# List work behind the attention of a step, output weights loaded by SyncE, last activation finished behind the next pair's copy: one change to a tuned attention and two-layer kernel

## The chip, the cores and the metric

The kernel runs on one core of a Trainium2 chip. Its time is device microseconds of one execution. The kernel before took 919.52 us (median of three runs, 918.92 to 920.69). Five engines run their own instruction streams and meet at semaphores: TensorE (PE: matmuls into PSUM banks), VectorE (DVE), ScalarE (ACT), GpSimd (POOL) and SyncE (SP, which starts transfers). ACT and POOL can start transfers too; they then stand in that engine's own queue of instructions (ACTq in the profile).

## What is computed

```
ret  = (scale * q @ k.T  *  decay mask) @ v            # 4 batches, 8 heads, 576 tokens, 64 per head
x    = ret as 2304 tokens x 512
h    = x @ w_in;  g = h * sigmoid(1.702 h);  y = g @ w_out            # 512 -> 2048 -> 512
xn   = y / rms(y) * rms_g
gate = xn @ w_gate;  val = xn @ w_val
out  = (gate * sigmoid(gate) * val) @ w_out2                          # 512 -> 1536 -> 512
```

All tensors are float32.

## The kernel before

A float32 operand is held as a high and a low part; each product is three matmuls, high by high, high by low and low by high (`three`, L290 to L292). The parts are made by a rounding copy on ACT and a subtraction on DVE. The attention is computed in chunks with a running state, in 18 units of 128 tokens, and its pieces are laid between the matmuls of the first layer (`attend`: transposes, scores, `a_both` for scores of one unit with outputs of another, `a_out`). L420 (DVE) masks scores, L490 (ACT) and L494 (DVE) move an attention output out of PSUM; until L494 is through, the next hidden product finds no free bank.

The first layer runs over four blocks of tokens, n = 0 to 3. Blocks 0 to 2 have 16 steps f of one 128-wide slice of the hidden layer: attention piece, hidden product (`m1_up`), activation (L646, L626 on ACT, L628 on DVE), and the output product (`down`) of a step two back. Steps with `a_both` run one output product before the hidden product as well. Block 3 (768 tokens) runs in eight pairs of steps (`s_up`): seven half products with sums of the weights and of x in place of eight. L817 copies the first half product on ACT, L802 adds on DVE, `gelu` is L809 and L811 on ACT with L812 on DVE. The gated layer (`m2_up`) uses the same scheme in three blocks of twelve steps; its additions are L1085, its products L1088.

Beside this a list of work (`work`, filled by `in_prep` and `prep`) makes the weight sums ahead of time: load gate and val weights (L179), turn their bytes into words on ACT (`conv_words`, L199 and L200), join them on DVE (L253), add and subtract (L729, L743), split into parts (`split_off`: L716 on ACT, L717 on DVE) and store them (L721) to `sum_d` and `up_d`. `make(slot)` takes as much of the list at the end of a step as a table `room` gives that step. `split_off` goes round the buffers in `FILL[1]` and `FILL[2]` by a running count modulo their number. Output weights of the first layer that are no longer on the chip are loaded again by `w_rot` (L284, 512 KB each) on ACT's queue, into one of three slots. After a block come the norm's scaling (L941) and sums of normalised values for the next half products (L996 for block 0 of the gated layer, L1007 and L1014 for others), handed out by `spread` a few units at a time; at a block's last step (the edge) all that is left is run at once. `first_load` and `x_load` bring x back.

Order on each engine is the order in which this program emits the instructions; there is no scheduler.

Of the kernel before, what the change touches and what calls it, by code (L numbers as in the profile page):

```python
# [10 lines left out]
F32 = mybir.dt.float32  # L11
# [33 lines left out]
def kernel(  # L45
# [225 lines left out]
    def w_rot(n, f):  # L271


        at = A_ROT + (n * NF1 + f) % 3 * 1024
        both, wh, wl = fast[:, at:at + 1024], fast[:, at:at + 512], fast[:, at + 512:at + 1024]
        if ("out", f) in W:
            w = W["out", f][1]
            nc.scalar.copy(out=wh, in_=w)
            nc.vector.tensor_tensor(out=wl, in0=w, in1=wh.bitcast(F32), op=ALU.subtract)
            if n == 1 or f >= NKEEP:  # L280
                w_free("out", f)
                to_store.append(lambda: nc.sync.dma_start(out=out_d[f], in_=both.bitcast(F32)))
        else:
            nc.scalar.dma_start(out=both.bitcast(F32), in_=out_d[f])  # L284
        R["out", f] = (wh, wl)
# [491 lines left out]
    def s_up(p, downs, hook):  # L777
# [29 lines left out]
        def gelu(a, h, t):  # L807
            o = g_tile(TH)
            nc.scalar.activation(out=o, in_=a, func=AF.Gelu_apprx_sigmoid)  # L809
            gh, gl = (x[:, TH * t:TH * t + TH] for x in h)  # L810
            nc.scalar.copy(out=gh, in_=o)  # L811
            return lambda: nc.vector.tensor_tensor(out=gl, in0=o, in1=gh.bitcast(F32), op=ALU.subtract)  # L812

        c1, u2, u3 = side
        a = bank()
        product(a, 0, True)
        nc.scalar.copy(out=c1, in_=a)  # L817
        b = bank()
        product(b, 1, True)
        plus(u2, b, c1)  # L820
        product(a, 2, False)
        gelu(a, h0, 0)()
        hook(0)
# [5 lines left out]
        plus(u3, c, u3)  # L829
        gelu(u3, h1, 1)()  # L830
        hook(1)
        run(downs[1], KD)
        product(b, 5, False)
        plus(c1, b, c1)
        low = gelu(c1, h1, 0)
        product(c, 6, False)
        plus(u2, c, u2)
        low()
        gelu(u2, h0, 1)()

# [341 lines left out]
    with tc.manual_schedule():  # L1182
# [245 lines left out]
        for n, f in ((n, f) for n in (1, 2) for f in range(NF1)):  # L1428
            fn = gap.get((n, f), (None,))[0]
            length = 5.45 + {a_trans: 0.9, a_both: 2.2, a_out: 1.2}.get(fn, 0)  # L1430
            taken = 0.7 + {a_trans: 0.7, a_both: 3.5, a_out: 0.9}.get(fn, 0) + 0.7 * (n == 1 and 0 < f <= NKEEP)
            taken += 1.2 * (4 < f < 14) + (0, 3.8, 3.8, 1.9)[max(0, f - 12) * (n == 2)]
            room[n, f] = max(0, 0.85 * length - taken) * (0 if n == 1 and f < 2 else 0.7 if n == 2 and f < 9 else 1)
        for p in range(NF1 // 2):
            for i in range(2):
                room["last", 2 * p + i] = max(0, (4.8, 2.0)[i] - {0: 1, 1: 1.4, 11: 1.9, 12: 3.8, 13: 1.9, 14: 3.3, 15: 2.3}.get(2 * p + i, 0))

        def make(*slot):

            total = sum(w[0] for w in work)  # L1440
            budget = total * room[slot] / (sum(room.values()) or 1)
            del room[slot]
            slot_no[0] += 1
            while work and budget > work[0][0] / 2 and (len(work[0]) == 2 or work[0][2] in ready):
                cost, op = work.popleft()[:2]
                op()
                budget -= cost
            for f in [f for f in due if due[f] <= slot_no[0]]:
                del due[f]
                conv_words("gate", f)  # L1450
                conv_words("val", f)
                ready.add(f)

        out2_next = [0]
        for n in range(N1 - 1):
            for f in range(NF1):
# [27 lines left out]
                if n > 0 and f == 3:  # L1484
# [3 lines left out]
                    norm += [sq[a:b] for a, b in zip(cuts, cuts[1:])]  # L1488
                if n == 2:
                    if f == 11:  # L1490
                        assert not load_at and wfree == list(range(11)), wfree
# [8 lines left out]
                        sum_load(0)  # L1500
                    if f in (7, 12):
                        for i in range(2):
                            nc.sync.dma_start(
                                out=(fast[:, 4864 + 1536 * i:][:, :2 * TH] if f == 7 else late[:, (768, 5376)[i]:][:, :2 * TH])
                                .bitcast(F32).rearrange("p (k c) -> p k c", k=2),
                                in_=x_d[:, 2 * i:2 * i + 2, TH * (f // 12):][:, :, :TH],
                            )
# [4 lines left out]
                if joined:  # L1512
                    run(down(pending.pop(0)), KD)
                if (n, f) == (0, 0):


                    m1_up(n, f, lambda: conv_join([to_conv.pop(0)]), lambda: conv_words(*to_conv[0]))
                else:
                    m1_up(n, f, lambda: run(rows, 1))
# [4 lines left out]
                else:  # L1524
                    run(spread, 2)
                if n == 2 and f == 13:
                    held_ids = [sfree.popleft() for _ in range(2)]
# [4 lines left out]
                    }, temps, x1, True)  # L1532
                if n == 2 and f > 12:
                    run(sums, 4 if f < 15 else len(sums))
                pending.append((1, n, f))
                if len(pending) > LAG:
                    run(down(pending.pop(0)), KD)
                if n > 0:
                    make(n, f)
            if n == 0:  # L1540
                w_rot(n, NF1 - 1)
        assert not norm
        FILL[2].append(slots(11, 2))
        for s in range(1, NSUM):
            sum_load(s)
        side.extend(norm_tile(nm) for nm in ("c1", "u2", "u3"))
        for p in range(NF1 // 2):
            last = p == NF1 // 2 - 1

            def hook(i):  # L1550
                if i == 0 and p == 0:
                    x_split(temps[1], x1[XT4])
# [4 lines left out]
                if p > 4 and sums:  # L1557
                    run(sums, (0, 2, 4, 2, 2, 1)[2 * p + i - 10])
                if last and i == 0:
                    ring_load(1)  # L1560
                    ring_load(2)
                if last:
                    out2_make(i)
                make("last", 2 * p + i)
                if p > 4 and out2_next[0] < 2:
                    w_load("out2", out2_next[0])
# [3 lines left out]
            w_rot(N1 - 1, 2 * p)  # L1570
            if p == 5:
                held_ids = [sfree.popleft() for _ in range(2)]
                temps = [k_halves(stage(i)[:, :2 * TH]) for i in held_ids]
                raw = {
                    (0, 0): k_halves(fast[:, 16384:][:, :2 * TH]), (0, 1): x_parts(XT3)[1], (1, 0): x_parts(X10)[1],
                    (1, 1): x_parts(X11)[1],
                }
                raw = {k: t.bitcast(F32) for k, t in raw.items()}
                x_load(0, raw)
                sums = x_sums(raw, temps, [x_parts(i) for i in range(7)], False)  # L1580
            if p == 6:
# [13 lines left out]
        for n in range(NBLK):  # L1595
            for f in range(NF2):
# [28 lines left out]
                def hook(i, c=None):  # L1625
# [92 lines left out]
```

## Time and profile before

| | |
|---|---|
| median of three runs | 919.52 us |
| profiled execution | 921.01 us, span 919.3 us |
| mean granted TensorE clock | 0.984 of full speed |
| busy: PE, DVE, ACT, POOL | 884.9, 574.9, 393.1, 38.3 us |
| moved by DMA | 206.61 MB, mean 225 GB/s |

Block 0 to 2 of the first layer take the time to about 349 us, the pairs run to about 490, the gated layer from there on. In a row of the timeline the bracket holds how long the engine stood idle before the instruction, and what it was waiting for; `x` counts the instructions in a row. A row of the waits has the sum, the number and the longest. Matmul durations in the trace overlap, so spacing from start to start tells the pace.

### The profile page before, as it was taken

The numbers are of one execution on the slowest core, as the hardware profiler recorded it, in microseconds if no ns is written. First come the engines' busy times: TensorE is split into PE (matmuls) and PEld (weight loads), VectorE is DVE, ScalarE is ACT, GpSimd is POOL, SyncE is SP. The second block draws the span as 40 slices with busy tenths as digits, with TensorE's granted clock in tenths as the row PEclk, the third lists the DMA queues.
The fourth block names the chain that finished last, engine by engine and source line by source line (L and its number), as shares of the span: only waits on it lengthen the run. The fifth ranks groups of instructions, "written<-read, shape, count | busy, mean of one in ns | idle before, by whom it ended". The sixth has DMA issues, their size and how long they took to land.

```text
span 919.3 us, 16132 instructions
## 1 busy us (share of the span) xinstructions
PE 884.9 (96%) x6122; PEld 782.4 (85%) x6122; DVE 574.9 (63%) x1041; ACT 393.1 (43%) x748; POOL 38.3 (4%) x41
## 2 busy tenths in 40 slices
PE   8999999997988997999998999999999999999998
PEld 7778888885877886899887999989999999999997
DVE  4787746677754677675674567677565666444444
ACT  3777653433443555555454434335323225222222
POOL 2202111021000000000000000000000000000000
PEclk9999999998998998999999999999999999999999
DMA  9997946757898798999947866655855555655553
GB/s 215 247 298 227 253 132 224 247 168 239 259 343 282 218 323 287 339 353 307 349 144 264 270 204 195 206 161 183 275 160 161 161 160 171 219 161 160 161 161 103
DMA packets 166877, 206.61 MB, mean 225 GB/s; under 512 B 73420, under 2 KB 100304, under 8 KB 166800
## 3 DMA queue, kind: packets, MB, share of 16 engines
q1 hardware_dynamic: 160308, 183.68, 64.0%
q10 hardware_dynamic: 6364, 21.64, 6.9%
q8 instruction: 49, 0.80, 0.4%
q0 software_dynamic: 128, 0.27, 0.1%
q14 instruction: 28, 0.23, 0.1%
HBM read 154.15 MB, written 51.38 MB: 224 GB/s over the span
## 4 chain that ended last, share of the span: by engine, by line
PE 73%; DVE 10%; ACT 9%; DMA 5%; issue 2%; ACTq 0%; SPq 0%; POOL 0%; DVEq 0%; POOLq 0%
PE h L290 14%; PE h L292 13%; PE h L291 13%; PE acc L290 7%; PE acc L291 7%; PE acc L292 7%; DMA up_d<-tops 3%; PE v L292 2%; PE v L291 2%; PE v L290 2%; PE at L371 1%; DVE tops L729 1%; ACT sslots L200 1%; ACT g L809 1%; DMA sslots<-in_moe_w_val_dram 1%
## 5 line engine op out<-in xcount | busy, mean ns | idle before, releaser
L290 PE MATMUL h<-fast 128*128 128x384 f32 (+1 forms) x744 | 267.5, 360 | 25.5 <-DVE x L494 11.4
L291 PE MATMUL h<-fast 128*128 128x384 f32 (+1 forms) x744 | 263.1, 354 | 0.7 <-DVE fast L1007 0.7
L292 PE MATMUL h<-fast 128*128 128x384 f32 (+1 forms) x744 | 263.1, 354 | 0.0
L1085 DVE TENSOR_TENSOR tops<-h,tops 128x384 f32<-128x384 f32 x180 | 99.8, 556 | 146.3 <-PE h L292 144.2
L290 PEld LDWEIGHTS h<-fast 128*128 128x128 f32 x744 | 141.6, 190 | 42.8 <-DVE x L494 12.3
L291 PE MATMUL acc<-fast 128*128 128x512 f32 x400 | 157.8, 395 | 0.0
L291 PEld LDWEIGHTS h<-fast 128*128 128x128 f32 x744 | 141.7, 190 | 10.1 <-DVE fast L1007 0.9
L290 PE MATMUL acc<-fast 128*128 128x512 f32 x376 | 149.1, 397 | 0.0
L292 PEld LDWEIGHTS h<-fast 128*128 128x128 f32 x744 | 141.5, 190 | 8.2 <-DVE fast L228 0.2
L292 PE MATMUL acc<-fast 128*128 128x512 f32 x376 | 148.3, 394 | 0.0
L1118 ACT CAST fast<-g 128x384 fp32r<-128x384 f32 x36 | 18.5, 514 | 211.4 <-DVE g L1088 211.4
L291 PEld LDWEIGHTS acc<-fast 128*128 128x128 f32 x400 | 75.8, 189 | 11.9
L292 PEld LDWEIGHTS acc<-fast 128*128 128x128 f32 x376 | 71.2, 189 | 15.4
L290 PEld LDWEIGHTS acc<-fast 128*128 128x128 f32 x376 | 71.2, 189 | 12.6
L628 DVE TENSOR_TENSOR fast<-g,fast 128x512 fp32r<-128x512 f32 x48 | 34.4, 716 | 69.8 <-ACT fast L626 69.8
L716 ACT CAST tops<-tops 128x512 fp32r<-128x512 f32 (+1 forms) x58 | 34.0, 597 | 65.6 <-DVE tops L729 42.4
L646 ACT ACTIVATE g<-h 128x512 f32<-128x512 f32 x48 | 28.4, 592 | 73.1 <-PE h L292 69.0
L291 PE MATMUL v<-fast 128*128 128x512 f32 (+1 forms) x136 | 46.3, 340 | 0.0
L717 DVE TENSOR_TENSOR tops<-tops 128x512 fp32r<-128x512 f32 (+1 forms) x58 | 39.6, 696 | 8.9 <-ACT tops L716 7.3
L292 PE MATMUL v<-fast 128*128 128x512 f32 (+1 forms) x112 | 39.5, 352 | 0.0
L290 PE MATMUL v<-fast 128*128 128x512 f32 (+1 forms) x112 | 39.4, 351 | 0.0
L199 ACT ACTIVATE sslots<-sslots 128x512 f32<-128x512 f32 x56 | 37.6, 671 | 3.8 <-DMA sslots<-in_moe_w_gate_dram 3.1
(189 smaller groups left out, 1136.8 us busy)
## 6 DMA issues: line engine op xcount, KB each, us to landing
fast<-up_d SPq DMA_DIRECT2D x252, 256.0 KB, 3.0
fast<-out_d ACTq DMA_DIRECT2D x41, 512.0 KB, 4.0
up_d<-tops SPq DMA_DIRECT2D x78, 256.0 KB, 5.0
sslots<-in_moe_w_out_dram SPq DMA_DIRECT2D x18, 512.0 KB, 5.6
out_d<-fast SPq DMA_DIRECT2D x16, 512.0 KB, 5.6
sum_d<-tops SPq DMA_DIRECT2D x32, 256.0 KB, 3.4
sslots<-in_moe_w_in_dram SPq DMA_DIRECT2D x15, 512.0 KB, 6.1
fast<-sum_d SPq DMA_DIRECT2D x26, 256.0 KB, 4.6
```

The lines of the kernel that those rows point to most:

```text
L199: nc.scalar.activation(out=hi, in_=hi, func=AF.Prelu, scale=2.0 ** -112, alpha=-(2.0 ** 32))
L200: nc.scalar.activation(out=lo, in_=byte, func=AF.Copy, scale=1 / 32, bias=-31 / 64)
L290: nc.tensor.matmul(ps, lh, rh, start=first, stop=False, skip_group_check=more)
L291: nc.tensor.matmul(ps, lh, rl, start=False, stop=False, skip_group_check=more)
L292: nc.tensor.matmul(ps, ll, rh, start=False, stop=last, skip_group_check=more)
L371: nc.tensor.transpose((more if i == 0 and p > 1 else pt[i])[:, p * 128:(p + 1) * 128], t[:, 2 * p:2 * p + 2, :].rearrange("p h d -> p (h d)"),
L628: nc.vector.tensor_tensor(out=gl, in0=g, in1=gh.bitcast(F32), op=ALU.subtract)
L646: nc.scalar.activation(out=g, in_=ps, func=AF.Gelu_apprx_sigmoid)
L716: nc.scalar.copy(out=wh.bitcast(F32R), in_=w)
L717: nc.vector.tensor_tensor(out=wl.bitcast(F32R), in0=w, in1=wh, op=ALU.subtract)
L1085: nc.vector.tensor_tensor(out=o, in0=a, in1=b, op=ALU.add)
L1118: nc.scalar.copy(out=gh0, in_=g0)
```

## The change

The diff below is cut. `w_rot` issues its load on SyncE. In `s_up` the two last steps of the last activation (copy and subtraction) go to `left` and are run by `last_half` in the next pair (that function is there already for the gated layer). `make` comes right behind the output product in steps with `a_both`, and not at their end; conversions that are due are not run in such a step. The table `room` is new, and so is the number of sums of x per step. `FILL[2]` gets its fourth buffer at step 1 of block 2 and not at its end. In the first block of the gated layer five units of `spread` run per step instead of six.

```diff
@@ w_rot
-            nc.scalar.dma_start(out=both.bitcast(F32), in_=out_d[f])
+            nc.sync.dma_start(out=both.bitcast(F32), in_=out_d[f])
@@ s_up
-            nc.scalar.copy(out=gh, in_=o)
-            return lambda: nc.vector.tensor_tensor(out=gl, in0=o, in1=gh.bitcast(F32), op=ALU.subtract)
+            return (
+                lambda: nc.scalar.copy(out=gh, in_=o),
+                lambda: nc.vector.tensor_tensor(out=gl, in0=o, in1=gh.bitcast(F32), op=ALU.subtract),
+            )
...
         nc.scalar.copy(out=c1, in_=a)
+        last_half(0)
         b = bank()
         product(b, 1, True)
         plus(u2, b, c1)
+        last_half(1)
...
-        gelu(u2, h0, 1)()
+        left.extend(gelu(u2, h0, 1))
@@ room
-            taken = 0.7 + {a_trans: 0.7, a_both: 3.5, a_out: 0.9}.get(fn, 0) + 0.7 * (n == 1 and 0 < f <= NKEEP)
-            taken += 1.2 * (4 < f < 14) + (0, 3.8, 3.8, 1.9)[max(0, f - 12) * (n == 2)]
-            room[n, f] = max(0, 0.85 * length - taken) * (0 if n == 1 and f < 2 else 0.7 if n == 2 and f < 9 else 1)
+            taken = 0.7 * (fn is a_trans) + (0.9 if fn is a_out else 0) + 0.7 * (n == 1 and 0 < f <= NKEEP)
+            taken += (0.6 if f < 10 else 2.2) * (4 < f < 14) + (n == 2) * {12: 2.9, 13: 2.9, 14: 2.9, 15: 2.4}.get(f, 0)
+            if fn is a_both:
+                room[n, f] = 2.5
+            elif after is a_both:
+                room[n, f] = max(0, 2.8 - taken)
...
@@ make
-            for f in [f for f in due if due[f] <= slot_no[0]]:
+            for f in [f for f in due if due[f] <= slot_no[0] and gap.get(slot, (None,))[0] is not a_both]:
@@ steps of blocks 0 to 2
+                    if f == 1:
+                        assert len(work) <= 10 * NF2, len(work)
+                        FILL[2].append(slots(11, 2))
...
                 if joined:
                     run(down(pending.pop(0)), KD)
+                    if n > 0:
+                        make(n, f)
...
-                if n > 0:
+                if n > 0 and not joined:
                     make(n, f)
...
-                if n == 2 and f == 13:
+                if n == 2 and f == 12:
...
-                    run(sums, 4 if f < 15 else len(sums))
+                    run(sums, 3)
@@ pairs, hook
-                    run(sums, (0, 2, 4, 2, 2, 1)[2 * p + i - 10])
+                    run(sums, (4, 2, 3, 0, 2)[2 * p + i - 10])
...
-                if last:
-                    out2_make(i)
+                if p > 5 and i == 0:
+                    out2_make(p - 6)
@@ gated layer, hook
-                        while spread and spread[0] not in banked and ran[0] < 6:
+                        while spread and spread[0] not in banked and ran[0] < (6 if n else 5):
```

First place: DVE in step 14 of block 1, one with `a_both` (L941, the norm's scaling, is L946 in the change). Before:

```order
L717 TENSOR_TENSOR tops<-tops 128x2x256
L743 TENSOR_TENSOR tops<-fast 128x512 x2
L729 TENSOR_TENSOR tops<-tops 128x256 x2
L628 TENSOR_TENSOR fast<-g,fast 128x512
L941 SCALAR_TENSOR_TENSOR sslots<-sslots,rg,r 128x384 x4
L729 TENSOR_TENSOR tops<-tops 128x256 x2
L717 TENSOR_TENSOR tops<-tops 128x2x256 x2
L743 TENSOR_TENSOR tops<-fast 128x512
L420 TENSOR_TENSOR lows<-at,mask 128x4x64 x2
L494 TENSOR_TENSOR x<-at,x 128x128 x2
```

In the change:

```order
L743 TENSOR_TENSOR tops<-fast 128x512 x2
L729 TENSOR_TENSOR tops<-tops 128x256
L628 TENSOR_TENSOR fast<-g,fast 128x512
L946 SCALAR_TENSOR_TENSOR sslots<-sslots,rg,r 128x384 x4
L729 TENSOR_TENSOR tops<-tops 128x256 x2
L420 TENSOR_TENSOR lows<-at,mask 128x4x64 x2
L494 TENSOR_TENSOR x<-at,x 128x128 x2
L451 TENSOR_TENSOR S<-at,sdec 128x256
L729 TENSOR_TENSOR tops<-tops 128x256
L717 TENSOR_TENSOR tops<-tops 128x2x256 x2
L743 TENSOR_TENSOR tops<-fast 128x512
```

The two splits L717 and a sum L743 of the step now stand behind L494; two sums of the step are left ahead of it.

Second place: ACT in steps 1 and 2 of block 2 (step 2 has `a_both`; L683 copies the outputs of block 1 that are complete). Before:

```order
L646 ACTIVATE g<-h 128x512
L626 CAST fast<-g 128x512
L683 COPY sslots<-acc 128x512 x2
L716 CAST tops<-tops 128x2x256
L716 CAST ww<-tops 128x256
L490 COPY x<-at 128x256 x2
L284 DMA fast<-out_d 128x1024
```

In the change:

```order
L646 ACTIVATE g<-h 128x512
L626 CAST fast<-g 128x512
L683 COPY sslots<-acc 128x512 x2
L716 CAST tops<-tops 128x2x256
L199 ACTIVATE sslots<-sslots 128x512
L200 ACTIVATE sslots<-sslots 128x512
L199 ACTIVATE sslots<-sslots 128x512
L200 ACTIVATE sslots<-sslots 128x512
L490 COPY x<-at 128x256 x2
L716 CAST tops<-tops 128x2x256
L716 CAST tops<-tops 128x256
```

Four conversions now stand ahead of L490, behind an L716 whose buffer was written by the split just before it.

Third place: DVE at the edge of block 0 of the gated layer (L1085, L1088, L941, L996 are L1090, L1093, L946, L1001 in the change). Before:

```order
L996 TENSOR_TENSOR sslots<-sslots 128x768 x3
L1085 TENSOR_TENSOR tops<-h,tops 128x384 x2
L1088 TENSOR_TENSOR g<-tops,g 128x384
L1085 TENSOR_TENSOR tops<-h,tops 128x384
L1123 TENSOR_TENSOR fast<-g,fast 128x384
L1088 TENSOR_TENSOR g<-tops 128x384
L996 TENSOR_TENSOR sslots<-sslots 128x768
L1085 TENSOR_TENSOR tops<-h,tops 128x384
```

In the change:

```order
L946 SCALAR_TENSOR_TENSOR sslots<-sslots,rg,r 128x384
L1090 TENSOR_TENSOR tops<-h,tops 128x384 x2
L1093 TENSOR_TENSOR g<-tops,g 128x384
L1090 TENSOR_TENSOR tops<-h,tops 128x384
L1128 TENSOR_TENSOR fast<-g,fast 128x384
L1093 TENSOR_TENSOR g<-tops 128x384
L946 SCALAR_TENSOR_TENSOR sslots<-sslots,rg,r 128x384 x3
L1001 TENSOR_TENSOR sslots<-sslots 128x768 x4
L1090 TENSOR_TENSOR tops<-h,tops 128x384
```

Seven units of the norm and its sums now stand between the last product of one step and the first addition of the next, where one stood.

## Rows read from the trace of the kernel before

**Rows 1.** The page: busy time, share of the span, instructions of each engine.

```profile
PE 884.9 (96%) x6122; PEld 782.4 (85%) x6122; DVE 574.9 (63%) x1041; ACT 393.1 (43%) x748; POOL 38.3 (4%) x41
```

**Rows 2.** Waits of TensorE: us in total, times, longest.

```profile
PE h L290 <- DVE x L494: 11.4, 2, 6.4
PE h L290 <- ACT c L817: 6.7, 4, 3.6
...
PE h L290 <- DVE tops L1085: 1.5, 4, 0.4
...
PE h L290 <- DVE c L802: 0.7, 2, 0.5
```

**Rows 3.** Timeline of TensorE: start, us, instruction, idle time before.

```profile
226.59 0.79 PE L290 MATMUL h<-fast 128*128 128x512 f32 x1 [6.40 <-DVE x L494]
...
268.41 0.69 PE L403 MATMUL at<-lows 64*64 64x64 f32 x32
...
270.44 0.50 PE L290 MATMUL acc<-fast 128*128 128x512 f32 x1
...
278.46 0.79 PE L290 MATMUL h<-fast 128*128 128x512 f32 x1 [5.01 <-DVE x L494]
...
352.84 0.69 PE L290 MATMUL h<-fast 128*128 128x384 f32 x1 [3.60 <-ACT c L817]
...
452.40 0.44 PE L290 MATMUL h<-fast 128*128 128x384 f32 x1 [1.99 <-ACT c L817]
...
487.59 0.48 PE L290 MATMUL h<-fast 128*128 128x384 f32 x1 [3.16 <-issue]
```

**Rows 4.** Stretches: us, busy time and instructions by engine; granted clock; DMA share; GB/s.

```profile
226.60:234.00 7.40, 7.40 (x22) 5.89 (x23) 1.13 (x4) 1.22 (x2) 0.00 (x0) 0.65 0.92 259
...
278.50:286.00 7.50, 7.50 (x28) 6.10 (x29) 1.98 (x5) 2.36 (x5) 0.00 (x0) 0.70 0.55 145
352.90:360.00 7.10, 7.10 (x23) 6.24 (x24) 4.10 (x8) 3.04 (x6) 0.00 (x0) 0.63 0.92 312
452.40:460.00 7.60, 7.60 (x34) 6.76 (x35) 4.56 (x6) 2.57 (x4) 0.00 (x0) 0.78 0.74 282
...
626.00:634.00 8.00, 7.99 (x40) 6.92 (x40) 5.42 (x9) 3.41 (x5) 0.00 (x0) 1.00 0.42 123
```

**Rows 5.** Timeline of DVE ahead of the first gap.

```profile
219.23 2.20 DVE L941 SCALAR_TENSOR_TENSOR sslots<-sslots,rg,r 128x384 f32<-128x384 f32 x4
```

**Rows 6.** Timeline of ACT ahead of the second gap.

```profile
274.88 0.65 ACT L199 ACTIVATE sslots<-sslots 128x512 f32<-128x512 f32 x1 [3.10 <-DMA sslots<-in_moe_w_gate_dram]
...
277.46 0.62 ACT L490 COPY x<-at 128x256 f32<-128x256 f32 x2
```

**Rows 7.** Timeline of ACT ahead of the third gap.

```profile
343.17 0.59 ACT L646 ACTIVATE g<-h 128x512 f32<-128x512 f32 x1
...
351.58 0.62 ACT L716 CAST tops<-tops 128x512 fp32r<-128x512 f32 x1 [2.35 <-DVE tops L729]
```

**Rows 8.** Timeline of ACT ahead of the fourth gap.

```profile
451.87 0.48 ACT L817 COPY c<-h 128x384 f32<-128x384 f32 x1 [1.82 <-DMA up_d<-tops]
```

**Rows 9.** Timeline of DVE ahead of the fifth gap.

```profile
486.94 0.55 DVE L802 TENSOR_TENSOR c<-h,c 128x384 f32<-128x384 f32 x1
```

**Rows 10.** DMA issues: count, KB of one, median us from issue to landing.

```profile
fast<-out_d ACTq DMA_DIRECT2D x41, 512.0 KB, 4.0
up_d<-tops SPq DMA_DIRECT2D x78, 256.0 KB, 5.0
...
sslots<-in_moe_w_gate_dram SPq DMA_DIRECT2D x12, 512.0 KB, 6.6
```

**Rows 11.** Waits of SyncE's queue: us in total, times, longest.

```profile
SPq L721 <- DVE tops L717: 89.7, 28, 11.1
```

**Rows 12.** Timeline of DVE at the edge of block 0 of the gated layer.

```profile
618.53 2.81 DVE L996 TENSOR_TENSOR sslots<-sslots 128x768 f32<-128x768 f32 x3
...
624.87 0.95 DVE L996 TENSOR_TENSOR sslots<-sslots 128x768 f32<-128x768 f32 x1
625.74 0.55 DVE L1085 TENSOR_TENSOR tops<-h,tops 128x384 f32<-128x384 f32 x1
```

More of the change, by code (lines that the diff above doesn't have):

```diff
@@ L820, in s_up @@
         plus(u2, b, c1)
+        last_half(1)
         product(a, 2, False)
-        gelu(a, h0, 0)()
+        run(list(gelu(a, h0, 0)), 2)
         hook(0)
@@ L829, in s_up @@
         plus(u3, c, u3)
-        gelu(u3, h1, 1)()
+        run(list(gelu(u3, h1, 1)), 2)
         hook(1)
@@ L834, in s_up @@
         plus(c1, b, c1)
-        low = gelu(c1, h1, 0)
+        high, low = gelu(c1, h1, 0)
+        high()
         product(c, 6, False)
@@ L1428 @@
         for n, f in ((n, f) for n in (1, 2) for f in range(NF1)):
-            fn = gap.get((n, f), (None,))[0]
-            length = 5.45 + {a_trans: 0.9, a_both: 2.2, a_out: 1.2}.get(fn, 0)
-            taken = 0.7 + {a_trans: 0.7, a_both: 3.5, a_out: 0.9}.get(fn, 0) + 0.7 * (n == 1 and 0 < f <= NKEEP)
-            taken += 1.2 * (4 < f < 14) + (0, 3.8, 3.8, 1.9)[max(0, f - 12) * (n == 2)]
-            room[n, f] = max(0, 0.85 * length - taken) * (0 if n == 1 and f < 2 else 0.7 if n == 2 and f < 9 else 1)
+            fn, after = (gap.get((n, f + i), (None,))[0] for i in range(2))
+            taken = 0.7 * (fn is a_trans) + (0.9 if fn is a_out else 0) + 0.7 * (n == 1 and 0 < f <= NKEEP)
[4 more added lines that the diff above has]
+                room[n, f] = max(0, 2.8 - taken)
+            else:
+                room[n, f] = max(0, 0.85 * (5.45 + 0.9 * (fn is a_trans)) - 0.7 - taken)
+            if n == 1 and f < 2:
+                room[n, f] = 0
         for p in range(NF1 // 2):
             for i in range(2):
-                room["last", 2 * p + i] = max(0, (4.8, 2.0)[i] - {0: 1, 1: 1.4, 11: 1.9, 12: 3.8, 13: 1.9, 14: 3.3, 15: 2.3}.get(2 * p + i, 0))
+                taken = {0: 1, 1: 1.4, 10: 3.8, 11: 1.9, 12: 4.2, 14: 3.3, 15: 2}.get(2 * p + i, 0)
+                room["last", 2 * p + i] = max(0, (4.2, 1.4)[i] - taken)
         def make(*slot):
@@ L1500 @@
                         sum_load(0)
-                    if f in (7, 12):
+                    if f in (7, 11):
                         for i in range(2):
@@ L1505 @@
                                 .bitcast(F32).rearrange("p (k c) -> p k c", k=2),
-                                in_=x_d[:, 2 * i:2 * i + 2, TH * (f // 12):][:, :, :TH],
+                                in_=x_d[:, 2 * i:2 * i + 2, TH * (f // 11):][:, :, :TH],
                             )
@@ L1532 @@
                     }, temps, x1, True)
-                if n == 2 and f > 12:
-                    run(sums, 4 if f < 15 else len(sums))
+                if n == 2 and f > 11:
+                    run(sums, 3)
                 pending.append((1, n, f))
@@ L1542 @@
         assert not norm
-        FILL[2].append(slots(11, 2))
         for s in range(1, NSUM):
@@ L1550, in hook @@
             def hook(i):
+                nonlocal held_ids, temps, sums
                 if i == 0 and p == 0:
@@ L1557, in hook @@
                 if p > 4 and sums:
-                    run(sums, (0, 2, 4, 2, 2, 1)[2 * p + i - 10])
+                    run(sums, (4, 2, 3, 0, 2)[2 * p + i - 10])
+                if (p, i) == (4, 1):
+                    held_ids = [sfree.popleft() for _ in range(3)]
+                    *temps, first_x = [k_halves(stage(i)[:, :2 * TH]) for i in held_ids]
+                    raw = {(0, 1): x_parts(XT3)[1], (1, 0): x_parts(X10)[1], (1, 1): x_parts(X11)[1]}
+                    raw = {(0, 0): first_x, **{k: t.bitcast(F32) for k, t in raw.items()}}
+                    x_load(0, raw)
+                    sums = x_sums(raw, temps, [x_parts(i) for i in range(7)], False)
                 if last and i == 0:
@@ L1561, in hook @@
                     ring_load(2)
-                if last:
-                    out2_make(i)
+                if p > 5 and i == 0:
+                    out2_make(p - 6)
                 make("last", 2 * p + i)
-                if p > 4 and out2_next[0] < 2:
+                if p > 4 and out2_next[0] < 2 and len(sfree) > 0:
                     w_load("out2", out2_next[0])
@@ L1570 @@
             w_rot(N1 - 1, 2 * p)
[L1571 to L1580, printed above, removed]
             if p == 6:
```

## The prediction, made before the changed kernel was run

> **What bounds the kernel now.** I read the engine shares first: TensorE is busy 884.9 of 919.3 us, so all its idle time is 34.4 us [rows 1]. Only what shortens those gaps, or the slow matmuls behind them, can move the end. The waits of TensorE say who ends the gaps [rows 2]: L494, the DVE addition that closes an attention output (11.4 us in two waits), L817, the ACT copy of a pair's first half product (6.7 in four), and small ones. The timeline of TensorE puts them in place [rows 3]: it restarts at 226.59 after 6.40 us, at 278.46 after 5.01, at 352.84 after 3.60, at 452.40 after 1.99, and at 487.59 after 3.16 for which the profile has no releaser. Together 20.2 us. The start of the kernel, which the change leaves alone, holds much of the rest, and after about 610 us there is no gap before the last few matmuls.
>
> The table by stretches adds a second cost [rows 4]. Behind each large gap TensorE's granted clock is partly at the lower of its two levels (1.2 instead of 2.4 GHz): 0.65 over 7.40 us, 0.70 over 7.50, 0.63 over 7.10, 0.78 over 7.60. What is missing to full speed is 0.35 x 7.40 = 2.6, then 2.3, 2.6 and 1.7 us. A stretch without a gap before it (626 to 634) has 1.00. So a gap of 2 to 6 us costs its length and some 1.6 to 2.6 us more. For the fifth, of 3.16 us, I take 1.7, the smallest of the four. The five together cost 20.2 + 10.9 = 31.1 us.
>
> **What the change removes.** I take its parts in the order of the program.
>
> Gap 1 (226.59). DVE was behind: ahead of L420 and L494 it had sums, splits and four L941 of 0.55 each [rows 5], and ACT's L490 stood behind four conversions. By the new order the list's splits and sums of this step stand behind L494, and nothing of the list on ACT is ahead of L490. DVE keeps L628, four L941, two sums, two L420 and two L494, eleven instructions, by the 0.55 of an L941 some 6 us, within the 8.0 us that TensorE has itself to do there (worked out at place A). So I cost this gap at zero: minus 6.40 and 2.6 = -9.0. TensorE's own matmuls are the cover; were the four L941 2.2 us late, 0.4 us of gap would come back.
>
> Gap 2 (278.46). ACT was held: its conversion L199 waited 3.10 us for a gate load, and L490 came behind all four conversions, 2.58 us after the first [rows 6]. In the changed step these stand behind L490. Minus 5.01 and 2.3 = -7.3. Two other attention steps now have conversions or DVE joins ahead of L490 and L420. By the durations of [rows 5, 6] each is 0.2 to 0.6 us late; with DMA traffic that the list's earlier start draws forward I charge +2.0 for them (0 to 4).
>
> Gap 4 (452.40). ACT's queue stood at the issue of an output-weight load, and the copy L817 behind it waited 1.82 us [rows 8] for an older store. The issue now stands on SyncE, so ACT is free: minus 1.99 and 1.7 = -3.7. SyncE takes 41 issues. They wait there for the weight slot to be read, as they did on ACT, and everything behind them in SyncE's queue waits along: list stores, attention loads, gate loads. An output load is wanted two steps later, at least four runs of twelve matmuls (3.0 us each, worked out at place A), and lands in 4.0 [rows 10], which is the cover.
>
> Gap 5 (487.59). DVE had L253 and L1062 of the next weights ahead of L802 at 486.94 [rows 9]. They now come a pair earlier; a table load on ACT remains ahead of the last activation's copy, 0.5 us. Minus 3.16 and 1.7 plus 0.5 = -4.4.
>
> Smaller waits. L817's 6.7 us are 3.60 + 1.99 and two short ones of together 1.1; L802 has 0.7 and L1085 1.5 [rows 2]. With the last activation's copy behind the next pair's L817, and five units instead of six on DVE per step, I take 1.3 of the 1.8 and 1.3 of the 1.5: -2.6.
>
> **What it adds.** Three places where the new order itself makes a wait.
>
> Place A, step 2 of token block 2. ACT has there L716, four conversions and only then L490. This L716 writes the buffer that was filled a step before, since the ring of buffers grows by one there and the index jumps; so it waits for the two stores of that buffer. They go out about 1.9 us into the step's first matmuls (behind an output load on SyncE). TensorE has then two runs of twelve output matmuls and the attention before it needs L494: attention 268.41 to 270.44, outputs 270.44 to 273.45 (the restart at 278.46 less its 5.01) [rows 3], so 3.0 + 2.0 + 3.0 = 8.0 us after the first of them, which leaves 6.1 us from the issue. Stores of this kind land in 5.0 us [rows 10]; L716 takes 0.6 [rows 7], the conversions 2.6 at most [rows 6], and from L490's start to TensorE's restart it is 1.0 (277.46 to 278.46): 9.2. The gap is some 3.1 us, plus 2.0 for the clock: +5.0 in round numbers. If the stores land in 3 us the gap is 1.1 and the clock may hold (+1); at 7 us it is 5.1 + 2.6 (+8).
>
> Place B, the start of the pairs (gap 3). Before, ACT's last L716 waited 2.35 us for DVE and L817 followed [rows 7]. In the new order two L716 and four conversions stand ahead of that copy. The gate load that the conversions need waits on SyncE for a DVE join of the last step to free its staging place, so it goes out late, by DVE's order some 2 us after the last activation L646 (four instructions of 0.55, an estimate), and lands after 6.6 [rows 10]. With the conversions (2.6) and the copy (0.5) TensorE restarts 11.7 us after L646, where it was 352.84 - 343.17 = 9.7. Net +2.0 (0 if the load lands in 4.6 us, +4.5 at 9); the clock is already low there.
>
> Place C, the last step of the first block of the gated layer. At most five units of the spread list now run in a step, and what is left runs in one burst at the edge. DVE then has three L941 and four L996 ahead of the L1085 that was at 625.74, where it had one L996; the other three stood earlier [rows 12]. L941 is 0.55, L996 0.94 (2.81 for three): 3 x 0.55 + 3 x 0.94 = +4.5 us for L1085, which releases the bank of the fourth half product. TensorE was not idle there before (7.99 of 8.00 us busy [rows 4]) and has nothing else in its order, so the gap is 4.5. The clock adds 2.1, between the least and the most above: +6.6 (4.5 to 7.1).
>
> **Sum.** -9.0 - 7.3 + 2.0 - 3.7 - 4.4 - 2.6 + 5.0 + 2.0 + 6.6 = -11.4 us. The profiled execution took 921.0 us (span 919.3), 1.5 above the median of 919.5. I set the sum against each: 921.0 - 11.4 = 909.6 for a like execution, 919.5 - 11.4 = 908.1 for the median. I forecast 908.
>
> **Rivals.**
> (1) The new waits A and B don't come, because the stores and the gate load land sooner in stretches that the change leaves emptier. For it: 4.0 us is the middle for output loads of twice a store's size [rows 10]. Against: at the two gaps where they matter the conversions waited for just such loads [rows 6]. It gives 908.1 - 5.0 - 2.0 = 901.
> (2) None of the three places bites, and the small charge goes too: 908.1 - 5.0 - 2.0 - 6.6 - 2.0 = 892.5. Against it: place C is counted in instructions of one engine, in order, with nothing to hide them.
> (3) Loads land later. 41 output loads of 512 KB now stand in one queue with the gate loads, and a gate load issued right behind one lands up to 4.0 us later [rows 10]. Place B has exactly that order. Then B costs 4.0 more, and places like it in block 2 some 2: 908.1 + 6 = 914.
> The Trainium skill speaks for this one ("DMA: Bandwidth & Descriptors", sections "Issuing engines are not separate DMA queues" and "Queues, rings and completion order"): loads started from several engines share the same DMA engines and save only issue time, while each DMA engine takes turns between the queues that have work. By that rule the output loads lose the turns of a queue of their own; the trace agrees so far as their 4.0 us against 6.6 for equal gate loads goes. By it the sum would be 914, by the row of the output loads alone 908.
> (4) Slower than before: output loads come too late for their matmuls. SyncE's queue stands 89.7 us in all behind one DVE line, L717, at most 11.1 us at once [rows 11]; an output load behind such a store is issued 11.1 us late, lands 6.6 later, and misses a slack of two steps (four runs of 3.0 us) by 5.7. With the clock (2.2) each costs 8. From two such loads on the gain is spent: 908.1 + 16 = 924. Against it: the long stands fall where the list has little to do, and two loads would have to meet them.
> (5) The order does not act as read, since gaps 1 and 2 stay for another reason (DVE late at the same place through the norm): 908.1 + 9.0 = 917.
>
> **How the numbers follow.** Forecast (904 to 912) 0.58, rival 1 0.13, rival 2 0.07, rival 3 0.13, rival 4 0.05, rival 5 0.04. The range that leaves out no more than 2 in 10 takes in rivals 1 and 3 and the bounds of A to C: 898 to 915. A measurement of this kernel can tell about 0.2% (1.8 us) from no change. Faster by more than that (below 917.7): all but rival 4 and part of 5, 0.92. Within 0.2%: 0.03, slower 0.05.
>
> **What would show it.** Right: no wait for L494 near 220 to 227 and 273 to 279, no ACT load issues and none of the waits at 452 and 487; a wait for L494 of 2 to 5 us in the first attention step of block 2 with ACT's L716 held by a store; a wait for the pair copy (now L819) of 4 to 8 us at the start of the pairs; a wait for L1090 (the old L1085) of about 4.5 us near 620, each with the granted clock low behind it. Wrong: TensorE waiting for an output load, the two old gaps still there, or no gap near 620.

## The result, and the profile after

The changed kernel took 910.25 us (median of four runs, 908.08 to 911.28) against 919.22 for the kernel before (four runs): ratio 0.9897, 95% interval 0.9874 to 0.9921, so about 1% faster. The forecast was 908 with a range of 898 to 915. Between the medians the change is -9.0 us, where the sum of the prediction was -11.4. The profiled execution, 908.08 us with a span of 906.4, is the fastest of the four; that of the kernel before, 921.01, lies above all four of its runs. So the two traces are 12.9 us apart, 4.0 more than the medians.

The waits of TensorE (us in total, times, longest), which answer to [rows 2]:

```profile
PE h L290 <- ACT x L490: 6.4, 1, 6.4
PE h L290 <- ACT c L819: 4.6, 2, 4.2
PE h L290 <- DVE tops L1090: 4.3, 1, 4.3
```

Three waits stand where five did. L819 and L1090 are the old L817 and L1085. L490 is the ACT copy just ahead of L494. The timeline of TensorE has the places, answering to [rows 3]:

```profile
219.63 0.50 PE L290 MATMUL h<-fast 128*128 128x512 f32 x1 [0.30 <-DVE x L494]
251.50 0.79 PE L290 MATMUL h<-fast 128*128 128x512 f32 x1 [6.37 <-ACT x L490]
344.15 0.69 PE L290 MATMUL h<-fast 128*128 128x384 f32 x1 [4.21 <-ACT c L819]
610.88 0.69 PE L290 MATMUL h<-fast 128*128 128x384 f32 x1 [4.33 <-DVE tops L1090]
```

The first row is where gap 1 was: 0.30 us are left of 6.40. No row of over 0.6 us comes in the stretches of gaps 2, 4 and 5. The other three are places A, B and C of the prediction. The stretches behind them (columns as in [rows 4]) show the clock at its lower level for part of the time, and full where gap 1 was:

```profile
219.60:227.00 7.40, 7.37 (x32) 6.12 (x33) 3.72 (x8) 3.58 (x6) 0.00 (x0) 1.00 0.63 190
251.50:259.00 7.50, 7.50 (x31) 6.16 (x32) 5.42 (x11) 2.93 (x6) 0.00 (x0) 0.79 0.95 311
344.10:351.60 7.50, 7.45 (x23) 6.46 (x24) 4.29 (x8) 2.88 (x5) 0.00 (x0) 0.59 1.05 400
611.00:618.50 7.50, 7.50 (x23) 6.36 (x24) 4.31 (x6) 0.83 (x1) 0.00 (x0) 0.63 0.11 35
```

Missing to full speed are 0.21 x 7.5 = 1.6 us behind A, 3.1 behind B and 2.8 behind C.

What held each place is read on the other engines. ACT at place A:

```profile
239.77 0.62 ACT L716 CAST tops<-tops 128x512 fp32r<-128x512 f32 x1 [4.99 <-DMA sum_d<-tops]
...
248.37 0.62 ACT L716 CAST tops<-tops 128x512 fp32r<-128x512 f32 x1 [5.86 <-DMA up_d<-tops]
...
251.10 0.61 ACT L490 COPY x<-at 128x256 f32<-128x256 f32 x2
```

DVE's half of the split that the first of these L716 begins:

```profile
240.42 0.69 DVE L717 TENSOR_TENSOR tops<-tops 128x512 fp32r<-128x512 f32 x1 [2.51 <-ACT tops L716]
```

SyncE's queue there: the two stores of that split from 241.14 on, then an output load.

```profile
241.14 1.10 SPq L721 DMA_DIRECT2D up_d<-tops  x2
242.33 0.66 SPq L284 DMA_DIRECT2D fast<-out_d  x1
```

So the first L716 waits 4.99 us for an older store, to `sum_d`; its split is ready at 241.11, and the stores go out at once. They are issued by 242.24 and have landed when the second L716 starts at 248.37, after 6 to 7 us; this L716, four conversions and L490 follow without another wait. The DMA engines are full there (share 1.01 in the table by stretches):

```profile
244.00:256.00 12.00, 5.63 (x19) 4.13 (x19) 5.43 (x12) 4.36 (x9) 0.00 (x0) 0.72 1.01 364
```

At place B SyncE's queue shows the gate load at 336.96, with nothing issued for almost 10 us before it:

```profile
326.98 0.32 SPq L284 DMA_DIRECT2D fast<-out_d  x1
336.96 0.38 SPq L179 DMA_DIRECT2D sslots<-in_moe_w_gate_dram  x1
```

ACT there, with the gate load and the val load ending its waits:

```profile
335.15 0.60 ACT L646 ACTIVATE g<-h 128x512 f32<-128x512 f32 x1 [1.12 <-PE h L292]
...
340.44 0.66 ACT L199 ACTIVATE sslots<-sslots 128x512 f32<-128x512 f32 x1 [2.45 <-DMA sslots<-in_moe_w_gate_dram]
...
342.54 0.65 ACT L199 ACTIVATE sslots<-sslots 128x512 f32<-128x512 f32 x1 [0.90 <-DMA sslots<-in_moe_w_val_dram]
...
343.64 0.46 ACT L819 COPY c<-h 128x384 f32<-128x384 f32 x1
```

DVE at place C (seven units, ahead of the addition that TensorE waits for), answering to [rows 12]:

```profile
606.67 3.68 DVE L1001 TENSOR_TENSOR sslots<-sslots 128x768 f32<-128x768 f32 x4
610.27 0.55 DVE L1090 TENSOR_TENSOR tops<-h,tops 128x384 f32<-128x384 f32 x1
```

And the issues of the whole run (KB of one, median us to landing), answering to [rows 10]:

```profile
fast<-out_d SPq DMA_DIRECT2D x41, 512.0 KB, 6.1
...
sslots<-in_moe_w_gate_dram SPq DMA_DIRECT2D x12, 512.0 KB, 6.8
```

### The profile page after: what moved, and what is told of

Read it like the earlier page. It is cut to its first block, busy times and chain, and to the rows that moved or that the text cites. A ratio compares the mean times of both kernels' runs of the same rounds, so it can differ in the third digit from the quotient of the medians.

```text
span 906.4 us, 16125 instructions
## 1 busy us (share of the span) xinstructions
PE 879.8 (97%) x6122; PEld 780.2 (86%) x6122; DVE 571.4 (63%) x1041; ACT 392.1 (43%) x748; POOL 37.3 (4%) x41
## 4 chain that ended last, share of the span: by engine, by line
PE 80%; DVE 8%; DMA 5%; ACT 4%; issue 1%; SPq 1%; POOL 0%; DVEq 0%; ACTq 0%; POOLq 0%
PE h L290 15%; PE h L292 14%; PE h L291 14%; PE acc L290 8%; PE acc L291 8%; PE acc L292 8%; PE v L292 2%; PE v L291 2%; PE v L290 2%; PE at L371 2%; DMA sslots<-in_moe_w_val_dram 1%; PE at L482 1%; DMA up_d<-tops 1%; DVE tops L729 1%; DMA fast<-y_d 1%
## 5 line engine op out<-in xcount | busy, mean ns | idle before, releaser
L1090 DVE TENSOR_TENSOR tops<-h,tops 128x384 f32<-128x384 f32 x180 | 100.1, 556 | 149.4 <-PE h L292 147.6
L716 ACT CAST tops<-tops 128x512 fp32r<-128x512 f32 (+1 forms) x58 | 33.9, 599 | 60.3 <-DVE tops L729 30.0
L646 ACT ACTIVATE g<-h 128x512 f32<-128x512 f32 x48 | 28.6, 596 | 49.7 <-PE h L292 49.4
L717 DVE TENSOR_TENSOR tops<-tops 128x512 fp32r<-128x512 f32 (+1 forms) x58 | 37.3, 661 | 14.8 <-ACT tops L716 13.2
```

The source lines that it names most:

```text
L646: nc.scalar.activation(out=g, in_=ps, func=AF.Gelu_apprx_sigmoid)
L716: nc.scalar.copy(out=wh.bitcast(F32R), in_=w)
L717: nc.vector.tensor_tensor(out=wl.bitcast(F32R), in0=w, in1=wh, op=ALU.subtract)
L1090: nc.vector.tensor_tensor(out=o, in0=a, in1=b, op=ALU.add)
```

## Experiments

Ratios are to the kernel before, run beside them on the same chip. The kernel before was at 921.4 to 921.9 us there, 2 us above the runs so far, so ratios are compared and not times.

**e1, the ring at place A.**

```diff
+                        old, made = FILL[2], n_made[2]
+                        FILL[2] = [None] * 4
+                        FILL[2][made % 4] = slots(11, 2)
+                        for j in range(3):
+                            FILL[2][(made + 1 + j) % 4] = old[(made + j) % 3]
-                        FILL[2].append(slots(11, 2))
...
```

The cut leaves out that stores not yet issued are now kept by buffer and not by index.

> The changed kernel with one edit: when the ring FILL[2] grows to four buffers, it is put in an order in which the next split takes the new buffer and the oldest of the others come after it. Theory (store wait): at place A the L716 of step 2 of block 2 waits for two stores issued just before, and the four conversions and L490 stand behind it. Without that wait the gap of 6.4 us there is under 1 us and the slow clock behind it (0.79 over 7.5 us, 1.6 us) is gone: 910.2 - 7.5 = 902.7 us, 901.5 to 905. Rival (conversions): the four conversions ahead of L490, or the val load that the third of them reads, end the gap; then 3 us or more of it stay and the time is 906 to 910.

907.4 us, ratio 0.9861 (0.9832 to 0.9889). The gap at A is gone, and with it the doubt on the conversions, which still stand ahead of L490. But a new wait came 20 us later:

```profile
249.38 0.50 PE L290 MATMUL h<-fast 128*128 128x512 f32 x1 [0.42 <-ACT x L490]
270.54 0.79 PE L290 MATMUL acc<-fast 128*128 128x512 f32 x1 [4.31 <-DMA fast<-out_d]
```

TensorE waits for an output load there. In the 18 us before that load SyncE's queue never waits longer than 1.0 us; stores stand before the load, and then attention loads:

```profile
263.34 1.25 SPq L346 DMA_DIRECT2D lows<-in_v_dram  x1
264.64 2.08 SPq L284 DMA_DIRECT2D fast<-out_d  x2
```

The load goes out at 264.64 and TensorE wants it at 266.23; in the changed kernel, with the gap at A, it goes out at 262.25 and is wanted at 269.72. So gap A was also the time in which this queue caught up. The expected 7.5 us were won at A and most of them lost again: by the ratios the net gain against the changed kernel is some 3 us, and the two intervals overlap.

**e5, e1 with the output loads in ACT's queue.**

```diff
-            nc.sync.dma_start(out=both.bitcast(F32), in_=out_d[f])
+            nc.scalar.dma_start(out=both.bitcast(F32), in_=out_d[f])
```

> The changed kernel with the reordered ring of the run before (e1) and the output-weight loads in ACT's queue. In e1 the gap at place A went, and 20 us later TensorE waited 4.31 us for an output load that SyncE issued behind stores and attention loads. Theory (queue order): from ACT the same load goes out when its slot is free, so that wait is under 1 us and gap A stays under 1 us: ratio to before 0.981 to 0.984, some 902 to 905 us. Rival (transport): from 232 to 272 the DMA engines are busy all the time in before, in the changed kernel and in e1 (share 1.0 and more), so what is late is bytes and not a place in a queue; then 3 us or more of waits for a load or store stay between 240 and 280, and the ratio is 0.985 to 0.990.

906.84 us, ratio 0.9834 (0.9788 to 0.9880). The intervals of e1 and of the changed kernel overlap with this one, so the time does not tell them apart; the traces tell what became of the wait. No wait for a load is left between 240 and 280, and place C stays:

```profile
246.95 0.50 PE L290 MATMUL h<-fast 128*128 128x512 f32 x1 [0.33 <-ACT x L490]
...
610.24 0.69 PE L290 MATMUL h<-fast 128*128 128x384 f32 x1 [4.32 <-DVE tops L1091]
```

The load that came late in e1, the thirteenth of the 41, now goes out 13 us earlier:

```profile
251.28 0.33 ACTq L284 DMA_DIRECT2D fast<-out_d  x1
```

The bytes are the same in both, so the load was late by its place in SyncE's queue. The rival on transport falls for this wait. Small waits stand against it, 2.7 us in three for L494 and 2.6 in three for L803 (the old L802). But executions differ by about as much: e2, which has the changed kernel's program up to place C, has 2.0 and 2.2 there.

**e4, only the output loads back in ACT's queue.** The same edit in the changed kernel.

> The changed kernel with the output-weight loads (L284) back in ACT's queue. Theory (ACT held at the issue): the wait at the pairs' copy near 440 comes back with about 2 us and its slow clock, some 3.7 us, and waits of the pairs' copies of together 1 us; against it stores at place A go out somewhat sooner (1 us): 912 to 915 us. Rival (one queue): with a queue of their own the output loads land in 4.0 instead of 6.1 us and the gate loads in less as well, the gaps at A and B shrink by 2 us each with part of their clock, and it comes out at 906 to 910.

910.91 us, ratio 0.9900 (0.9872 to 0.9928): no difference from the changed kernel's 0.9897. Neither theory holds. Gap 4 did not come back, and the gaps at A and B did not shrink, though output loads land in 5.1 us here and in 6.1 from SyncE. Waits for L802 are 3.1 us for 0.5, but e2, which has the loads on SyncE and differs from the changed kernel only behind 600 us, has 2.2 of them before that, so executions differ by as much:

```profile
PE h L290 <- ACT x L490: 6.8, 1, 6.8
PE h L290 <- ACT c L819: 5.1, 2, 4.7
...
PE h L290 <- DVE c L802: 3.1, 3, 1.5
```

**e7, only the output loads moved, in the kernel before.** The diff of `w_rot` alone.

> The kernel before with one edit: output-weight loads from SyncE. Theory (ACT held at the issue): the gap at 452 goes (2.0 us and 1.7 of clock) and the others stay: ratio 0.995 to 0.997. Rival (slower): the loads are late behind list stores, TensorE waits for them in blocks 1 and 2: ratio over 1.0. Rival (no effect): the copy waits for something else there and the ratio is 0.998 to 1.002.

917.35 us, ratio 0.9959 (0.9935 to 0.9983). Gap 4 goes and the others stay; gap 2 is shorter by 2.2 us and gap 1 by 0.9, and a wait of 1.77 us for L802 comes in at 461.52. So the ratio is the one expected, but more than gap 4 is in it:

```profile
226.36 0.80 PE L290 MATMUL h<-fast 128*128 128x512 f32 x1 [5.55 <-DVE x L494]
275.97 0.80 PE L290 MATMUL h<-fast 128*128 128x512 f32 x1 [2.85 <-DVE x L494]
349.40 0.45 PE L290 MATMUL h<-fast 128*128 128x384 f32 x1 [3.38 <-ACT c L817]
...
481.03 0.66 PE L290 MATMUL h<-fast 128*128 128x384 f32 x1 [3.17 <-issue]
```

With e4: in the old order of the list the move of the loads is enough to remove gap 4, and in the new order it is not needed.

**e8, only the place of the list's work, in the kernel before.**

```diff
                 if joined:
                     run(down(pending.pop(0)), KD)
+                    if n > 0:
+                        make(n, f)
...
-                if n > 0:
+                if n > 0 and not joined:
                     make(n, f)
```

The condition on due conversions goes with it, so two things are changed here.

> The kernel before with one part of the change: in steps with scores and outputs the list's work comes behind the step's output product (ahead of its hidden product) and due conversions are not run there; table, ring, loads and the rest as before. Theory (engines' order): gaps 1 and 2 (6.4 and 5.0 us, with 4.9 of clock) go, 16 us in all, and no new one of over 2 us comes in blocks 1 and 2: ratio 0.981 to 0.985. Rival (table): since the table gives these steps next to nothing, the work lands in other steps' ends and one attention copy still comes late; one gap of 3 to 6 us stays and the ratio is 0.987 to 0.993.

916.5 us, ratio 0.9929 (0.9907 to 0.9950). The rival was right: gap 2 goes, gap 1 stays with 4.13 us.

```profile
223.81 0.80 PE L290 MATMUL h<-fast 128*128 128x512 f32 x1 [4.13 <-DVE x L494]
...
457.58 0.44 PE L290 MATMUL h<-fast 128*128 128x384 f32 x1 [3.07 <-DVE c L802]
```

On DVE ahead of gap 1 the splits L717 of the step before are still in front of L420 and L494, and ACT's L716 waits for DVE as in before, with four conversions of that step behind it and ahead of L490:

```profile
219.48 0.62 ACT L716 CAST tops<-tops 128x512 fp32r<-128x512 f32 x1 [6.20 <-DVE tops L729]
```

So gap 1 needs more than the new place. The new table gives the step ahead of an attention step little work and is the likely rest, but that is argued from the order: no run has the table alone. The old table also puts the list's end into the pairs, where DVE is late. L802 holds TensorE there for 3.07 us and, at 475.23, for 2.14. Ahead of these waits the same matmul starts 14.3 us earlier than in the kernel before (442.38 for 456.68); at the end 5.9 us are left. So the ratio of e8 is set by the pairs as much as by gap 1.

**e6, six units per step at place C.**

```diff
-                        while spread and spread[0] not in banked and ran[0] < (6 if n else 5):
+                        while spread and spread[0] not in banked and ran[0] < 6:
```

> The changed kernel with six units of the spread list per step in the first block of the gated layer, as before. Theory: the leftover burst at the edge is again one sum, the gap of 4.33 us near 611 and its slow clock go (7.1 us), and the short waits of the steps before (2.3 us between 550 and 625) come back: net -4.8 us against the changed kernel, ratio 0.983 to 0.986. Rival (another cause): the burst stays since the list itself starts later or ends later than in before, and the ratio stays near 0.990.

905.2 us, ratio 0.9814 (0.9768 to 0.9860), so the theory held: the burst made the gap. The wait for L1090 falls from 4.3 us in one to the four short ones of before:

```profile
PE h L290 <- DVE tops L1090: 1.5, 4, 0.4
```

**e2, the burst of place C moved behind the next addition.** The line `run(spread, len(spread))` goes from the start of the edge step into its `hook(2)`, ahead of the first four splits of x.

> The changed kernel with one edit: at the last step of block 0 of the gated layer the seven units left over (three scalings, four sums) run behind the addition for the fourth half product and not ahead of the first addition. Theory (DVE burst): the gap of 4.33 us near 611 goes, since 60 output matmuls (13 us) now cover the burst, and the clock of 0.63 over 7.5 us behind it (2.8 us): 910.2 - 7.1 = 903.1 us, 902 to 905. Rival (splits late): the burst only delays the next block's splits of x (L1012), and a gap of about the same size comes back at the next additions or at the first product of block 1: 908 to 911.

908.68 us, ratio 0.9873 (0.9841 to 0.9904). The rival was right: the gap moved from 610.88 to 621.35 and fell by only 0.8 us.

```profile
621.35 0.69 PE L290 MATMUL h<-fast 128*128 128x384 f32 x1 [3.55 <-DVE tops L1090]
```

```profile
613.67 3.68 DVE L1001 TENSOR_TENSOR sslots<-sslots 128x768 f32<-128x768 f32 x4
617.27 3.56 DVE L1012 TENSOR_TENSOR fast<-sslots,fast 128x768 fp32r<-128x768 f32 x4
```

I had the cover wrong: 18 output matmuls (4.1 us) stand there and not 60. DVE lacks time in the whole step, so the work has to go to earlier steps, as in e6.

**e3, conversions behind the pair's copy at place B.**

```diff
-            for f in [f for f in due if due[f] <= slot_no[0] and gap.get(slot, (None,))[0] is not a_both]:
+            for f in [f for f in due if due[f] <= slot_no[0] and gap.get(slot, (None,))[0] is not a_both and slot != (2, NF1 - 1)]:
```

> The changed kernel with one edit: conversions that are due are not run in the last step of block 2 but in the first slot of the pairs, behind the copy of the first half product. Theory (gate load): at place B the copy L819 stands behind four conversions that wait for their loads (2.45 and 0.90 us). The gap of 4.21 us at 344 is under 1.5 us, and the clock behind it (0.59 over 7.5 us, 3.1 us) mostly back: 910.2 - 5.5 = 904.7 us, 903 to 907. Rival (list late): the list then runs a slot behind in the first pairs, ACT is held there by the same loads and the additions or the pair copies wait instead: 908 to 912.

914.12 us, ratio 0.9923 (0.9896 to 0.9951): no gain. The copy is free, and TensorE waits instead for a load of weight sums, and later for an addition, since the list is behind:

```profile
349.78 0.66 PE L290 MATMUL h<-late,fast 128*128 128x384 f32 x1 [4.05 <-DMA fast<-sum_d]
457.47 0.44 PE L290 MATMUL h<-fast 128*128 128x384 f32 x1 [3.49 <-DVE c L802]
```

**e9, three edits together.** e1, e5 and e6 in one kernel.

> The changed kernel with three edits of the runs before: the ring reordered (e1), the output-weight loads in ACT's queue (e5), six units per step in the gated layer's first block (e6). Theory (the two places are independent): e5's gain and the removal of the edge gap add up, 0.9834 x 0.995 = 0.978 to 0.980, some 901 us; of gaps over 1.5 us only the one at the start of the pairs stays (4 to 5 us). Rival: with the edge gap gone something late behind it shows (the splits for block 1, or loads), and the ratio stays at 0.983 or more.

902.62 us, ratio 0.9786 (0.9761 to 0.9812), the fastest of all: 2.1% under the kernel before and, by the ratios, 1.1% under the changed one. The ratio is the one expected. The measured ratios of e5 and e6 would multiply to 0.975, so the gains may not add up in full; the intervals of e5 and e6 are too wide to settle it, and that of e6 overlaps with this one. The start of the pairs is the only large gap:

```profile
340.11 0.69 PE L290 MATMUL h<-fast 128*128 128x384 f32 x1 [4.84 <-ACT c L820]
```

**e10, e9 with place B taken apart.** The edit of e3, and the five loads of sums issued at the end of the last step of block 2, ahead of its `make`:

```diff
+                if (n, f) == (2, NF1 - 1):
+                    for s in range(1, NSUM):
+                        sum_load(s)
```

> As e9, and at the start of the pairs the due conversions run behind the copy of the first half product (e3), and the five loads of weight sums that the first pair needs are issued ahead of the last step's list work and not behind it. In e3 the gap moved from the copy to such a load, which stood behind a gate, a val and an output load. Theory (load order): with the sums loaded first, the gap of 4 to 5 us and the slow clock behind it (3 us) go, ratio 0.970 to 0.974, some 894 us. Rival (bytes): sum loads, gate loads and stores still take turns, and a wait of 3 us or more for a load or for an addition (L802) stays in the first two pairs: ratio 0.976 to 0.981.

904.8 us, ratio 0.9824 (0.9786 to 0.9861): not better than e9, with overlapping intervals. The wait for the pair's copy is gone, but TensorE waits 3.81 us for a load of sums instead, and 3.49 for L803 at 453.76, which is what the rival said. The edit did not do what I wrote. SyncE still issues the gate and val loads first, as the step before puts them there, and the five sum loads go out over 6.18 us:

```profile
334.06 0.38 SPq L179 DMA_DIRECT2D sslots<-in_moe_w_gate_dram  x1
...
336.20 6.18 SPq L769 DMA_DIRECT2D fast<-sum_d  x5
```

```profile
344.65 0.66 PE L290 MATMUL h<-late,fast 128*128 128x384 f32 x1 [3.81 <-DMA fast<-sum_d]
```

Four of the five are issued by 338.69. The fifth waits for an output load that ACT issued at 334.96; in the trace the two use the same completion semaphore (waits of SyncE's queue from 333 to 343):

```profile
SPq L769 <- DMA fast<-out_d: 3.4, 1, 3.4
```

The first sum load goes out 4.6 us before TensorE stops for one of them, against 4.2 in e3, and lands 8.3 us after its issue. So the edit won 0.5 us for it. Whether place B can be freed stays open; with the sums first it was not tried.

## Why the prediction was right, point by point

The time and the mechanism held: two kinds of gap taken away, three places where the new order makes a wait. The steps below are read from the two profiled executions. The lead is how much earlier the same work starts on TensorE in the changed kernel than in the kernel before; a step measures by how much it grows or falls. In all it comes to 12.9 us, of which 0.3 at the start of the kernel and 0.5 near 161 us belong to no step of the prediction.

- Gap 1: forecast -9.0, measured -8.5 (the lead grows from 0.85 to 9.35 us). DVE's eleven instructions ran inside TensorE's own time, as bounded; 0.30 us were left. e8 adds that the place of `make` alone does not do it.
- Gap 2: -7.3 forecast, -7.4 measured (0.7 to 8.1). e8 shows that the new place of `make`, with the condition on due conversions, removes it. The charge of +2.0 for two other attention steps was not needed in this execution, with 0.30 us of waiting for L494 in the whole kernel. It is not empty: in the traces of e2 and e6, which share the program up to place C, these waits come to 2.0 and 0.8.
- Place A: +5.0 forecast, +8.6 measured (9.35 down to 0.7), the step of the sum that was most off. The mechanism is shown by e1. Two terms were too small, by about the same. I had the stores go out 1.9 us after the first of the output matmuls; that one starts at 236.99 and they went out at 241.14, after 4.15 us, since their split waited for an L716 that was itself held by an older store. And I took the 5.0 us of [rows 10] for the landing: L716 started 7.2 us after the first issue, in a stretch where the DMA share is over 1.0 in before too (1.02 from 244 to 256). From L716 to the restart it took 3.1 us for the 4.2 assumed. The gap was 6.37 for 3.1; my bound for a landing in 7 us was 5.1 and +8.
- Place B: +2.0 forecast, -0.6 measured. TensorE restarts 9.0 us after L646, where it was 9.7 and I had 11.7. The wait is there with its cause (gate load behind the join, 1.8 us after L646 for the 2 assumed; e3 shows that the conversions hold the copy). The load landed 3.5 us after its issue, not 6.6; SyncE had issued nothing for almost 10 us before it, and the DMA share from 325 to 337 is 0.18. The wait itself grew, from 3.60 to 4.21; the lead grows all the same, since a wait of 0.69 us for L1007 just ahead of it, at 347.06 in before, is gone. Had I read the landings by place and not as one median, A would have come out dearer and B cheaper.
- Gaps 4 and 5 and the small waits: -10.7 forecast, -11.2 measured from the pairs to the step before place C. e7 shows gap 4's cause in the old order. That ACT's issue was what had to go is only half true, as e4 shows: the new order alone suffices. No run takes gap 5 by itself; that nothing waits there is read from the trace after only.
- Place C: +6.6 forecast, +7.1 measured (4.33 and 2.8 of clock). e6 removes it.
- Rival 4 (output loads too late on SyncE) gave nothing in the changed kernel, but e1 shows it is real: it was hidden behind gap A. The cover that I named, two steps of output matmuls, is not enough where attention loads and stores fill SyncE's queue.
- Rival 3: output loads landed in 6.1 us instead of 4.0 [rows 10], which is what the rival said; gate loads had 6.8 for 6.6. The queue is not the only cause. With the move alone they landed in 5.6 (e7), and with the loads in ACT's queue in 5.3 (e8) and 5.1 (e4), so the later order counts too. At place B the gate load did not stand behind an output load: it went out at 336.96 and the output load at 338.04.
- The page beside rival 3 ("DMA: Bandwidth & Descriptors" of the Trainium skill, section "Issuing engines are not separate DMA queues") says that the engine that starts a load matters only for issue time. In e4 the time did not change, which agrees with the rule. Between e1 and e5 the time at which the load was issued was what mattered, 4.31 us of TensorE's waiting.

The errors at A (+3.6), B (-2.6), the charge (-2.0), gap 1 (+0.5), place C (+0.5) and the gaps of the pairs (-0.5) nearly cancel. With the 4.0 us by which the two traces lie further apart than the medians, 908 for 910.25 is partly luck.

## What to carry to other kernels

Reordering a full queue moves its waits. Follow each instruction that now stands earlier to the slowest thing that it waits for (here a store of the buffer just written, by an index modulo a ring that grew), and ask who stands behind it. When a gap is removed, ask what used the gap to catch up. Work that is spread over steps must come out even at the end, for what is left over runs in one burst at the worst place. A median landing time hid a factor of two here between full and idle stretches (3.5 us for a gate load at place B, 6.8 as the median), so read it at the place.

## What was not expected of the hardware

The clock lost 1.6 us behind the longest gap of the changed kernel (6.37 us) and 2.8 to 3.1 behind the two of 4.2 to 4.3. In [rows 4] the gap of 6.40 cost 2.6. So the loss did not grow with the gap within these rows. In e7 the low clock came late: after a gap of 3.38 us the first matmuls ran at full speed, and only 1.4 us into the work the spacing from start to start of 512-column matmuls rose, from 0.23 us (350.55 to 350.78) to 0.40 (to 351.18). The stretch has 0.78, a loss of 1.7 us, where the like gap of 3.60 in the kernel before cost 2.6 [rows 4]:

```profile
350.55 0.41 PE L290 MATMUL acc<-fast 128*128 128x512 f32 x1
350.78 0.60 PE L291 MATMUL acc<-fast 128*128 128x512 f32 x1
351.18 0.63 PE L292 MATMUL acc<-fast 128*128 128x512 f32 x1
```

```profile
349.40:357.00 7.60, 7.60 (x31) 6.65 (x32) 5.42 (x9) 3.37 (x6) 0.00 (x0) 0.78 0.83 274
```

SyncE's issues were not of one price: in the changed kernel the issue of an output load (L284) took 0.66 us at 242.33, where the DMA share from 244 to 256 is 1.01, and 0.32 at 326.98, where it is 0.18 from 325 to 337.
